# Moving constants and loads, adding a branch hint and a PSUM unit, and searching a new instruction order, in an attention and state-space kernel

## Chip, cores and metric

The kernel runs on one core of a Trainium2 chip. The metric is the device time of one execution in microseconds (us). The number given for a kernel is the median of its runs. A profile is one more execution, taken by the hardware profiler. Its span, from first to last instruction, is about 1.8 us shorter than the device time of the same kernel.

## The reference, cut to what matters

Two halves with separate inputs, concatenated along the last axis. All inputs are bf16, S = 2048 positions, D = 448.

```python
def _A_ref(x, wqkv, wo):          # sliding, dilated attention: 16 heads of 28, 8 keys at distance 0, 2, ... 14
    q, k, v = split_heads(x @ wqkv)
    logits = einsum("bhsd,bhswd->bhsw", q, gather(k)) * Dh ** -0.5     # masked where the position is negative
    o = einsum("bhsw,bhswd->bhsd", softmax(logits), gather(v))
    return merge_heads(o) @ wo

def _B_ref(x, Lambda, B, C, log_dt, Dskip):   # diagonal complex state space
    Lam_bar = exp(exp(log_dt) * Lambda)
    Bu = x @ (((Lam_bar - 1) / Lambda)[:, None] * B).T
    h[t] = Lam_bar * h[t - 1] + Bu[t]
    return 2 * real(h @ C.T) + x * Dskip

out = concatenate([_A_ref(...), _B_ref(...)], -1)
```

## The kernel before

The kernel is a list of work items ("nodes"), each with an estimated cost per engine, an earliest start and a rank. A small planner walks these estimates in time and gives each engine a fixed order. The ranks come from a search outside the kernel. For items that two engines can do (`"V"` is DVE, `"A"` is ACT), the planner also chooses the engine. So a change of costs, start times or ranks changes the order on every engine and moves items from one engine to another.

The loads at the head, all issued in this order:

```python
    V.memset(zz[:, 0:640], 0.0)                  # operand of the warm-up matmuls
    xbar_x(xA, xA2, 0, 128)                      # SP: transposing load of 128 columns of x
    ACT.dma_start(Wv[0:64, 3, :], ...)           # 56 KB
    ACT.dma_start(Wv[:, 0:3, :], ...)            # 336 KB
    xbar_x(xA, xA2, 128, 256)
    xbar_x(xA, xA2, 256, 384)
    xbar_x(xA, xA2, 384, 512)
    # ... four small vectors, on ACT and GpSimd ...
    for q in (1, 0):                             # K, then Q weights, on SP
        SP.dma_start(Wraw[:, 0:3, D * q:D * q + D], ...)
        SP.dma_start(Wraw[0:64, 3, D * q:D * q + D], ...)
    # ... six loads of B weights on SP ...
    xbar_x(xA, xA2, 512, 768)                    # the second half of x
    xbar_x(xA, xA2, 768, 1024)
    xbar_x(xB, xB2, 0, 512)
```

V is computed in nine blocks, Q and K in column pieces. The weights of Q and K are first copied to a padded layout, in four sets of five copies, each set on DVE or ACT as the planner decides:

```python
    def n_wp(e, q, z):                           # one set
        # ...
        f = V.tensor_copy if e == "V" else ACT.copy
        f(o[:, 0:3], i[:, 0:3])
        f(o[0:64, 3], i[0:64, 3])
        f(o[64:128, 3], i[0:64, 0])
        f(o[0:64, 4:7], i[64:128, 0:3])
        f(o[64:128, 4:7], i[0:64, 1:4])
```

GpSimd (POOL) builds constants (masks, ones, zeros). It also makes a one-element memset, the "tick", between the two parts of each V, Q and K unit, for which PE waits:

```python
    def relay(h):
        k = h["tick"] = G.memset(tick[:, 0:1], 0.0)
        behind(k, h["done"][0])
        behind(k, h["done"][1])
```

At the end come eight output blocks `y`, each with two halves (`pe0`, `pe1`) in one PSUM unit of two banks, their evictions and stores, a one-element matmul that checks the softmax sums, and a branch on its result around an exact version of the attention. It skips that part.

```python
        def pe0(e, ...):
            ps = h["ps"] = unit()
            # ... 11 matmuls into ps[:, 0]
        def pe1(e, ...):
            ps, hb, lo = h["ps"], hbuf(hf), 128 * (t % 4)
            # ... 11 matmuls into ps[:, 1]
    # ...
    bad = nc.values_load(flag[0:1, 0:1], min_val=0, max_val=128)
    main.close()
    with tc.If(bad > 0):
        exact_attention(tc, A_x, A_wqkv, A_wo, out)
```

## Time and profile before

| | before |
|---|---|
| device time, median of 3 runs | 144.92 us (143.94 to 145.28) |
| span of the profile | 142.9 us |
| PE busy | 128.0 us, 90% |
| PE idle from 5.4 to 22 us | 5.9 us |
| PE's end to the end of the span | 6.5 us |

The prediction below shows the totals, the PE and DVE slices and the gaps. Two more views of the kernel before complete them. The first is POOL's row in the slices of the page (40 equal slices of the span; each digit is the busy share in tenths). The second is the list of what PE waited for between 5 and 22 us (line, releaser, total us, times, longest).

```profile
POOL 6967585902000000000000000000000000000000
```

```profile
PE mm L532 <- DVE Kt L511: 2.7, 2, 1.8
PE mm L533 <- DVE Wv L495: 1.0, 1, 1.0
PE mm L533 <- DVE Wpad L505: 0.9, 1, 0.9
PE mm L532 <- DVE Wpad L501: 0.7, 1, 0.7
PE mm L532 <- DMA xA<-in_A_x_dram: 0.6, 1, 0.6
```

POOL is busy for the first eight slices (28 us) and nearly idle afterwards. All but one of PE's head waits end with DVE work: the eviction of K out of PSUM (`Kt`), the padded weight copies (`Wpad`) and the copies that complete V's weights (`Wv`). The last, 0.6 us, is for the first tile of x.

### The profile page before, as it was taken

The numbers are of one execution on the slowest core, as the hardware profiler recorded it, in microseconds if no ns is written. First come the engines' busy times: TensorE is split into PE (matmuls) and PEld (weight loads), VectorE is DVE, ScalarE is ACT, GpSimd is POOL, SyncE is SP. The second block draws the span as 40 slices with busy tenths as digits, with TensorE's granted clock in tenths as the row PEclk, the third lists the DMA queues.
The fourth block names the chain that finished last, engine by engine and source line by source line (L and its number), as shares of the span: only waits on it lengthen the run. The fifth ranks groups of instructions, "written<-read, shape, count | busy, mean of one in ns | idle before, by whom it ended". The sixth has DMA issues, their size and how long they took to land.

```text
span 142.9 us, 3792 instructions
## 1 busy us (share of the span) xinstructions
PE 128.0 (90%) x1537; PEld 71.5 (50%) x1542; DVE 108.0 (76%) x228; ACT 89.5 (63%) x117; POOL 23.4 (16%) x86
## 2 busy tenths in 40 slices
PE   6697649999999999999999999999999999999910
PEld 2142538766634645454544656465656555455510
DVE  0349999999886999999999998999999995300000
ACT  0228963699898766998877799866652345222220
POOL 6967585902000000000000000000000000000000
PEclk9999999999999999999999999999999999999997
DMA  3999999302977949133030030255341295521120
GB/s 54 279 203 279 203 159 207 58 0 50 120 155 146 242 94 187 37 68 61 0 61 0 0 63 0 47 141 168 82 93 64 70 186 189 196 69 64 64 70 8
DMA packets 40449, 15.15 MB, mean 106 GB/s; under 512 B 33004, under 2 KB 40364, under 8 KB 40428
## 3 DMA queue, kind: packets, MB, share of 16 engines
q1 hardware_dynamic: 39728, 14.23, 47.4%
q0 software_dynamic: 192, 0.23, 1.0%
q10 hardware_dynamic: 508, 0.40, 0.9%
q8 instruction: 14, 0.23, 0.7%
q14 instruction: 7, 0.06, 0.1%
HBM read 3.16 MB, written 3.67 MB: 48 GB/s over the span
## 4 chain that ended last, share of the span: by engine, by line
PE 66%; DVE 21%; DMA 3%; issue 3%; ACT 2%; ACTq 1%; POOL 0%; POOLq 0%
PE mm L532 22%; PE mm L754 10%; PE mm L890 8%; PE mm L897 7%; PE mm L892 4%; PE mm L852 4%; PE mm L714 4%; DMA Wv<-in_A_wqkv_dram 3%; DVE rs L788 3%; PE mm L533 2%; DVE ra L767 2%; DVE rb L768 2%; PE mm L692 2%; DVE Kt L511 2%; DVE O L721 2%
## 5 line engine op out<-in xcount | busy, mean ns | idle before, releaser
L702 ACT ACTIVATE P<-mm 128x896 bf16<-128x896 f32 (+1 forms) x36 | 31.5, 934 | 2.3 <-PE mm L696 2.3
L532 PE MATMUL mm<-xA,Wpad 64*128 64x256 bf16 (+1 forms) x168 | 27.2, 305 | 3.8 <-DVE Kt L511 2.7
L533 PE MATMUL mm<-xA,Wpad 64*128 64x256 bf16 (+1 forms) x168 | 27.0, 306 | 0.9 <-DVE Wpad L505 0.9
L509 ACT CAST ys<-mm 128x896 bf16<-128x896 f32 (+1 forms) x15 | 12.5, 857 | 23.2 <-PE mm L900 17.4
L754 PE MATMUL mm<-xB,WT 128*128 128x512 bf16 x93 | 22.2, 380 | 0.3
L540 POOL MEMSET tick<- 1x1 f32 x41 | 4.6, 111 | 95.3 <-PE mm L533 95.0
L532 PEld LDWEIGHTS <-Wpad 64*128 64x128 bf16 x168 | 15.1, 94 | 8.7 <-DVE Wpad L501 1.2
L533 PEld LDWEIGHTS <-Wpad 64*128 64x128 bf16 x168 | 14.7, 94 | 4.8 <-issue 3.6
L754 PEld LDWEIGHTS <-WT 128*128 128x128 bf16 x98 | 8.9, 98 | 10.6 <-issue 0.4
L533 PE MATMUL mm<-Wv,xA 64*128 64x448 bf16 x63 | 13.1, 349 | 1.0 <-DVE Wv L495 1.0
L532 PE MATMUL mm<-Wv,xA 64*128 64x448 bf16 x63 | 13.2, 350 | 0.7 <-DMA xA<-in_A_x_dram 0.6
L890 PE MATMUL mm<-C,h 128*128 128x448 bf16 x56 | 11.9, 353 | 0.3 <-ACT P L702 0.3
L897 PE MATMUL mm<-C,h 128*128 128x448 bf16 x56 | 11.9, 353 | 0.0
L509 ACT CAST Qt<-mm 128x512 bf16<-128x512 f32 (+1 forms) x11 | 7.9, 749 | 6.1 <-PE mm L533 5.9
L532 PE MATMUL mm<-wo,OT 64*128 64x448 bf16 x56 | 10.8, 349 | 0.0
L533 PE MATMUL mm<-wo,OT 64*128 64x448 bf16 x56 | 10.8, 349 | 0.0
L953 DVE TENSOR_SCALAR flag<-mm 1x1 int32<-1x1 f32 x1 | 0.1, 147 | 13.5 <-PE mm L950 13.5
L721 DVE TENSOR_TENSOR O<-mm,rcs 112x896 bf16<-112x896 f32 (+1 forms) x9 | 9.8, 1092 | 0.3
L509 ACT CAST u<-mm 128x1024 bf16<-128x1024 f32 (+1 forms) x7 | 6.3, 893 | 4.4 <-PE mm L754 4.4
L714 PEld LDWEIGHTS <-P 128*128 128x128 bf16 x288 | 8.2, 96 | 1.7 <-issue 0.8
L532 PEld LDWEIGHTS <-xA 64*128 64x128 bf16 x63 | 5.7, 94 | 6.6 <-issue 1.3
L714 PE MATMUL mm<-Vt,P 128*128 128x29 bf16 x288 | 8.7, 176 | 0.1
(175 smaller groups left out, 243.6 us busy)
## 6 DMA issues: line engine op xcount, KB each, us to landing
out_dram<-ys SPq DMA_DIRECT2D x15, 224.0 KB, 2.4
Wraw<-in_A_wqkv_dram SPq DMA_DIRECT2D x2, 336.0 KB, 4.4
wo<-in_A_wo_dram SPq DMA_DIRECT2D x2, 336.0 KB, 4.8
Wv<-in_A_wqkv_dram ACTq DMA_DIRECT2D x1, 336.0 KB, 4.4
natW<-in_B_B_re_dram SPq DMA_DIRECT2D x1, 336.0 KB
natW<-in_B_B_im_dram SPq DMA_DIRECT2D x1, 336.0 KB, 6.0
out_dram<-ys SPq DMA_DIRECT2D x2, 112.0 KB, 2.5
OT<-O SPq DMA_TRANSPOSE x9, 2.8
```

Source lines behind the costliest of these rows:

```text
L509: ACT.copy(o, i)
L532: x = PE.matmul(ps[:, a, 0:n], lhs(0, lo[i]), rhs(0, lo[i]), start=(i == 0), stop=(i == 6), skip_group_check=True)
L533: y = PE.matmul(ps[:, b, 0:n], lhs(64, hi[i]), rhs(64, hi[i]), start=(i == 0), stop=(i == 6), skip_group_check=True)
L540: k = h["tick"] = G.memset(tick[:, 0:1], 0.0)
L702: ACT.activation(P[:].rearrange("p s g q -> p g s q")[:, 2 * z:2 * z + 2, :, 0:n], h["s"][z][:, :, 0:4 * n].rearrange("p g (s q) -> p g s ...
L714: PE.matmul(av[:, par, 29 * hd:29 * hd + 29], hb_[par]["P"][:, hd // 4, hd % 4, :], Vt[:, par, b, hd, :], start=True, stop=True)
L721: V.tensor_tensor(O[0:n, :].rearrange("p (a h d) -> p a h d", a=2, h=H), avv[0:n, :, :, 0:DH], rc.unsqueeze(3).to_broadcast((n, 2, H, DH)) ...
L754: PE.matmul(ps[:, i, :], WT[:, j, 128 * m:128 * m + 128], xB[:, j, HALF * hf:HALF * hf + HALF], start=(j == 0), stop=(j == 6))
L852: PE.matmul(ps[0:n, i, 0:D], natW[:, m, D + 128 * k:D + 128 * k + n], lazy["C1"][:, m, :], start=(m == 0), stop=False, skip_group_check=True)
L890: PE.matmul(ps[:, 0, 0:D], hb[:, m, lo:lo + 128], lazy["C2"][:, m, :], start=(m == 0), stop=False, skip_group_check=True)
L892: PE.matmul(ps[:, 0, 0:D], xB[:, k, tk], Gm[:, k, :], start=False, stop=(k == 3), skip_group_check=True)
L897: PE.matmul(ps[:, 1, 0:D], hb[:, m, lo + 1:lo + 129], lazy["C1"][:, m, :], start=(m == 0), stop=False, skip_group_check=True)
```

## The change

The intent has four parts. (a) POOL's constants come after DVE's weight copies (earliest start 17 us, and cut into small pieces so that ticks fit between them), so that they no longer run beside those copies (beside a memset of POOL the same 128x672 copy took 1.50 and 0.84 us, apart from them 0.38). (b) All of x is loaded in eight tiles ahead of the B weights, so that PE has V blocks to do early. The Q and K weights go to ACT's queue. (c) The end: a prefetch hint for PE's branch, and a PSUM unit for each half of the last output block. (d) A new search of the ranks for these arrival times. Four C loads also move from POOL to SP, and two small vector loads from ACT to POOL (neither is shown in the diff).

```diff
-RANK = {"v": (67.97, 4.568), "q0": (138.6, -7.905), "q1": (-53.81, 27.558), "s": (-197.77, 32.213), ...
+RANK = {"v": (-66.31, 15.076), "q0": (294.15, -25.592), "q1": (-315.77, 68.252), "s": (340.5, 1.243), ...
     # (all 20 pairs differ)
+    ACT.dma_start(Wv[:, 0:3, :], ...)
     ACT.dma_start(Wv[0:64, 3, :], A_wqkv[384:448, 2 * D:3 * D])
-    ACT.dma_start(Wv[:, 0:3, :], ...)
-    xbar_x(xA, xA2, 128, 256)
-    xbar_x(xA, xA2, 256, 384)
-    xbar_x(xA, xA2, 384, 512)
+    for i in range(1, 4):
+        xbar_x(xA, xA2, 128 * i, 128 * i + 128)
     for q in (1, 0):
-        SP.dma_start(Wraw[:, 0:3, D * q:D * q + D], ...)
-        SP.dma_start(Wraw[0:64, 3, D * q:D * q + D], ...)
+        ACT.dma_start(Wraw[:, 0:3, D * q:D * q + D], ...)
+        ACT.dma_start(Wraw[0:64, 3, D * q:D * q + D], ...)
+    for i in range(4, 8):
+        xbar_x(xA, xA2, 128 * i, 128 * i + 128)
     # ... B weights ...
-    xbar_x(xA, xA2, 512, 768)
-    xbar_x(xA, xA2, 768, 1024)
-    xbar_x(xB, xB2, 0, 512)
+    for i in range(4):
+        xbar_x(xB, xB2, 128 * i, 128 * i + 128)
     # ...
-    gm = [node(f"gm{i}", {"G": c}, f, [], 3 + i) for i, (c, f) in enumerate(((1.3, g_m1), ...))]
-    g_1 = node("one", {"G": 1.3}, g_one, [], 10)
-    g_z = node("zer", {"G": 1.7}, g_zero, [], 11)
+    late = 17.0
+    for i, f in enumerate(gms):                  # 15 pieces
+        gm.append(node(f"gm{i}", {"G": 0.42}, f, gm[-1:], 4, at=late))
+    g_1 = [node(f"one{a}", {"G": 0.67}, ..., at=late) for a in range(2)]
+    g_z = [node(f"zer{i}", ..., at=late) for i in range(4)]
     # ... estimated costs and start times adjusted, the weight copies from 10.8/11.8 to 8.5/10.0 ...
         def pe0(e, ...):
-            ps = h["ps"] = unit()
+            if t == 6:
+                tc.mark_branch_hint_location("exact", engines=(mybir.EngineType.PE,))
+            ps = h[0] = h[1] = unit()
         def pe1(e, ...):
+            if t == 7:
+                h[1] = unit()
-    with tc.If(bad > 0):
+    with tc.If(bad > 0, label="exact"):
```

## The prediction

> **What bounds the kernel now.** I read the page's totals and slices first, then the busy time of each engine by stage, then the PE timeline where it has gaps, then DVE and POOL beside those gaps, and last the end of the span. From the page:
>
> ```profile
> span 142.9 us, 3792 instructions
> PE 128.0 (90%) x1537; PEld 71.5 (50%) x1542; DVE 108.0 (76%) x228; ACT 89.5 (63%) x117; POOL 23.4 (16%) x86
> ...
> PE   6697649999999999999999999999999999999910
> ...
> DVE  0349999999886999999999998999999995300000
> ...
> PE 66%; DVE 21%; DMA 3%; issue 3%; ACT 2%; ACTq 1%; POOL 0%; POOLq 0%
> ```
>
> PE is full from slice 7 to slice 37, and it alone is full in the last sixth. It has holes in the first six slices, and there DVE is full. The stages, cut at the end of the warm-up matmuls (5.4 us), at the last hole and at PE's last matmul:
>
> ```profile
> 5.40:22.00 16.60, 10.71 (x131) 6.50 (x131) 13.70 (x41) 9.94 (x18) 11.44 (x32) 1.00 1.09 219
> 22.00:136.40 114.40, 113.21 (x1398) 63.61 (x1400) 93.81 (x187) 77.33 (x96) 7.92 (x41) 1.00 0.43 92
> 136.40:142.90 6.50, 0.05 (x1) 0.00 (x0) 0.15 (x1) 0.97 (x2) 0.00 (x0) 0.86 0.15 43
> ```
>
> The columns are length, then PE, weight load, DVE, ACT, POOL. PE is idle 5.9 us in the first stage and 1.2 us in the second; 6.5 us follow PE's end. So there are about 12 us in all that are not matrix work after the warm-up, and half lie in the head. The holes (PE timeline, idle before and releaser in brackets):
>
> ```profile
> 7.40 0.35 PE L533 MATMUL mm<-Wv,xA 64*128 64x448 bf16 x1 [1.04 <-DVE Wv L495]
> 13.82 0.28 PE L532 MATMUL mm<-xA,Wpad 64*128 64x256 bf16 x1 [0.73 <-DVE Wpad L501]
> 14.96 0.28 PE L533 MATMUL mm<-xA,Wpad 64*128 64x256 bf16 x1 [0.86 <-DVE Wpad L505]
> 18.96 0.27 PE L532 MATMUL mm<-xA,Wpad 64*128 64x256 bf16 x1 [1.75 <-DVE Kt L511]
> 21.50 0.27 PE L532 MATMUL mm<-xA,Wpad 64*128 64x256 bf16 x1 [0.94 <-DVE Kt L511]
> ```
>
> The last four are one cause: PE ran out of V blocks (only four of nine, since only 512 columns of x were loaded early), and then waited for DVE, which had the padded weight copies and the PSUM evictions in one queue. What slowed DVE, DVE and POOL lines of the same stretch:
>
> ```profile
> 12.26 1.50 DVE L501 COPY Wpad<-Wraw 128x672 bf16<-128x672 bf16 x1
> 15.95 0.84 DVE L501 COPY Wpad<-Wraw 128x672 bf16<-128x672 bf16 x1
> 18.83 0.38 DVE L501 COPY Wpad<-Wraw 128x672 bf16<-128x672 bf16 x1
> 12.19 1.32 POOL L351 MEMSET Vt<- 128x288 bf16 x1
> 15.73 0.82 POOL L355 MEMSET P<- 128x256 bf16 x3
> ```
>
> The same copy takes 0.38 us alone and 1.50 or 0.84 us when a POOL memset began just before it.
>
> [...] the first copy ends at 13.76, 0.25 us after the memset's end at 13.51, although the copy itself needs 0.38. [...] PE's compare-and-branch at 137.26 lasts 3.42 us, those of ACT, POOL, DVE and SP 0.05 to 0.07. [...] the C loads that move from POOL to SP landed 8.3 us after issue[...], but nothing on the path waits for them.
>
> **The change, part by part.**
>
> *Start of V.* The large part of Wv is now issued first on ACT's queue. Before, it was issued at 1.42 and landed at 5.78, behind a 56 KB piece at 0.82. Swapped, it should land about 0.55 us earlier (the issue that it stood behind took 0.56). The three DVE shift copies (5.81 to 7.35) move with it, unless the first x tile, which PE took at 6.00, holds it. Gain 0.5.
>
> *Head.* Eight 128-column transposes of x come before the other operands, so all nine V blocks can run. A block is 14 matmuls, 7 pairs at 0.188 us, so 1.32 us, and x tiles come about as fast (four took 5.56 us to issue, 1.39 each). The built order interleaves V blocks with K and Q units (7 pairs at 0.11, 0.77 us), so PE waits neither for one nor for the other. The Wraw loads move to ACT's queue; the K part should land some 2 us earlier than now (issue about 2.0 and 4.4 us to landing, against 6.42), later if it shares bandwidth with x, so I take 8.5. The Q part is held behind a semaphore of Wv and comes about 10. The weight copies become two sets on DVE and two on ACT (before: three and one). A set on DVE without POOL costs 0.38 + 0.19 + 0.21 + 0.39 + 0.39 = 1.56; on ACT 0.74 + 0.38 + 0.38 + 0.75 + 0.75 = 3.0. DVE saves 6.9 - 2 x 1.56 = 3.8 us of busy time.
>
> I walked the new order by hand with these durations and four PSUM buffers. PE starts V at 6.85, has four V blocks until 12.1, three K units until 14, V4 until 15.9, waits 0.5 for a buffer that ACT frees after its second weight set, then runs to 28 with waits of 0.4, and 0.5 and 0.6 up to the first softmax. That is 2.0 us of waits. Before, the starts of the matmuls at the four holes (12.74, 13.82, 14.96; 16.94, 18.96; 20.29, 21.50) are 5.45 us apart; less ordinary spacing and with some small late starts, 5.4 lost. Gain 3.4.
>
> *Middle.* The matrix work itself is unchanged. The order has fewer V, K and Q units left as filler, because they were done earlier. ACT must do the 36 exponentials (31.5 us) and its evictions in about 5 us less; I count 54 us of ACT work in a 60 us stretch. DVE's list after the first rotation shrinks by 2.9 us (two evictions of 1024 columns at 1.22, one of 896 at 1.09, less 0.66 for one of 512), and its last h piece, 119.88 now against the use of h at 121.84, should be ready at about 115. So neither becomes the end bound, but with three engines over 90% full some new waits will appear. I take 0.6 lost.
>
> *Tail.* The last block's two halves get a PSUM unit each. Now the eviction of the first half waits for the last matmul:
>
> ```profile
> 136.43 0.97 ACT L509 CAST ys<-mm 128x448 bf16<-128x448 f32 x2 [2.70 <-PE mm L900]
> ...
> 136.99 0.84 SPq L908 DMA_DIRECT2D out_dram<-ys  x2
> ```
>
> With its own unit the first half leaves under the second half's matmuls, and the last store is issued one eviction earlier: gain 0.43 (second eviction begins 136.43 instead of 136.86). The hint: SP's closing waits begin when the last store has landed (140.77), and PE's long branch ends at 140.69, so the branch alone is hidden. But 13 of that store's 16 pieces land by 139.21 and three only at 140.17, 140.52 and 140.77, and three instruction fetches (16 KB for 1.07 us, 8 KB for 0.56 and 0.65) lie just then in the DMA records. If PE's fetch goes earlier, the stragglers partly vanish. At most 1.5 us; the two 8 KB fetches probably belong to other engines and stay; the hint stands in the built program at the very start of PE's stream, not at the seventh block, so it may be spent long before the branch. I take 0.6.
>
> *Sum.* 0.5 + 3.4 - 0.6 + 0.43 + 0.6 = 4.3 us; 144.92 - 4.3 = 140.6.
>
> **Rivals.** (1) DVE, not PE, is the true limit: the chain of waits runs through DVE from 10 to 21 and from 44 to 62 us. Then the head gain is given back between 40 and 90, and only DVE's own saving (3.8 + 2.9, less four V evictions at 1.09 moved to it) counts: 2.3 us or so, and with the tail 141.6. For: DVE busy 93.8 of 114.4. Against: in the second stage PE is idle 1.2 us only. (2) Bandwidth: x, Wv and Wraw together are 2.3 MB before 8.5 us, near 290 GB/s, and the busiest slices show 279. If x tiles and weights come 2 us later than I think, the holes stay as waits for DMA, and half the head gain goes: 142.5. (3) The hint is without effect or hidden: 141.2. (4) Everything goes well, the stragglers vanish (1.5) and no new waits appear: 139.1.
>
> **Range and chances.** The rivals against it are worth +0.6 to +2 each and the one in favour -1.5, so 140.6 with 138.6 to 142.6 eight times in ten; the three times of before are themselves spread by 1.3 us. Faster by 2% means below 142.02; only rival 2, or 1 with 3, lands above. Faster 0.87, same 0.12, slower 0.01.
>
> **What would show it.** Right: PE busy in 5.4 to 22 rises from 10.7 to over 14 us; no Wpad copy over 0.5 us of the 128x672 form on DVE; POOL's constants lie after 17 us; PE's last matmul ends near 133 (now 136.4); its branch is short; the last store lands less than 2.5 us after issue (now 3.3). Wrong: PE holes put down to x or Wraw transfers before 15 us (rival 2); PE idle in the 22 to 133 stretch of well over 2 us, behind ACT's exponentials or DVE's rotations (rival 1); a PE branch of 3 us (rival 3). If the head gain appears but PE's end does not move with it, the order, not the head, is what I misjudged.

The 0.6 for the hint was the author's estimate: the DMA records of the kernel before show four instruction fetches near the end (at 138.26, 138.31, 138.54 and 141.46 us) but not for which engine, so "PE's fetch" and its link with the late pieces of the store were a theory, here and in the expectations of e1 to e4.

## The result and the profile after

A ratio here is the mean time of one kernel's fast runs over the mean of the other's fast runs of the same rounds, so it is not quite the ratio of the medians quoted.

| | before | after |
|---|---|---|
| device time, median of 4 runs | 144.59 us | 139.31 us (138.83 to 141.16, the longest a slow run) |
| ratio, 95% interval | 1 | 0.962 (0.955 to 0.969) |
| span | 142.9 us | 137.1 us |
| PE busy, share | 128.0 us, 90% | 128.6 us, 94% |

The page of the changed kernel: totals, three rows of slices (PE, DVE, POOL), and the chain of waits by engine.

```profile
span 137.1 us, 3790 instructions
...
PE 128.6 (94%) x1536; PEld 72.0 (53%) x1542; DVE 104.7 (76%) x222; ACT 93.0 (68%) x123; POOL 21.4 (16%) x85
...
PE   6959999999999999979999999999999999999970
...
DVE  0646986999996999999999999899999999500000
...
POOL 6500148889400000000000000000000000000000
...
PE 68%; DVE 11%; ACT 10%; DMA 5%; issue 2%; SPq 1%; DVEq 0%; ACTq 0%
```

PE is full from the fourth slice on, but for one slice of 7 tenths. DVE's share of the chain falls from 21% to 11%. POOL's block of work now lies in slices 6 to 11 and leaves the first weight copies alone. The stages, cut at the same places as in the prediction (PE's end is now 132.90), with length, then busy time of PE, weight load, DVE, ACT and POOL:

```profile
5.40:22.00 16.60, 15.06 (x176) 8.51 (x176) 11.04 (x36) 11.74 (x20) 3.56 (x22) 1.00 1.02 219
22.00:132.90 110.90, 109.39 (x1357) 62.00 (x1357) 92.16 (x184) 80.77 (x103) 13.62 (x53) 1.00 0.45 94
132.90:137.10 4.20, 0.07 (x1) 0.00 (x0) 0.15 (x1) 0.53 (x1) 0.00 (x0) 0.95 0.19 61
```

The first row must not be read as matrix work alone, because the warm-up matmuls (`tab`) reach into it. The clock records show the full clock from 4.50 us on in the profile before and from 6.97 after, and until then matmuls take longer (V's first one 0.55 us before 6.97, later ones 0.35). So the warm-up ended at 5.43 and at 6.22 us (start and length; first line before, second after):

```profile
1.34 4.09 PE L962 MATMUL mm<-tab 128*128 128x512 bf16 x11 [1.34 <-DVE tab L283]
1.34 4.88 PE L954 MATMUL mm<-tab 128*128 128x512 bf16 x11 [1.34 <-DVE tab L283]
```

So 0.8 us of the 15.06 are warm-up. This is chance and not the change: e1, e2 and e3 below have the same head, and their warm-up ended at 5.63, 5.61 and 5.34. The sum without it, counted in the records from V's first matmul (6.00 before, 6.15 after): PE is idle for 5.33 us before and 1.54 after up to 22 us, so 3.79 less. From there to its end it is idle for 1.51 us instead of 1.19, 0.32 more. Its busy time in both together is 123.84 and 123.67, so about the same. With V's start 0.15 later, PE's end comes 3.5 us earlier (136.40 to 132.90). What follows it shrinks from 6.50 to 4.20, 2.30 us. Together that is 5.8 us, the difference of the spans.

The head in detail: first the list of what PE waited for between 5 and 22 us, then two weight copies from DVE's timeline and the first of POOL's moved memsets from its timeline.

```profile
PE mm L516 <- DMA xA<-in_A_x_dram: 1.4, 1, 1.4
```

```profile
7.01 0.39 DVE L485 COPY Wpad<-Wraw 128x672 bf16<-128x672 bf16 x1 [0.56 <-DMA Wraw<-in_A_wqkv_dram]
15.65 0.38 DVE L485 COPY Wpad<-Wraw 128x672 bf16<-128x672 bf16 x1
...
18.87 0.20 POOL L324 MEMSET mst<- 32x128 bf16 x1
```

One wait is left, for the second tile of x. It landed at 9.03 us instead of 6.89, because the Q and K weights are now moved at the same time (h1 below shows this). Both 128x672 copies on DVE take 0.38 to 0.39 us. The evictions of the last output block, on ACT:

```profile
131.43 0.53 ACT L493 CAST ys<-mm 128x448 bf16<-128x448 f32 x1 [1.18 <-PE mm L881]
132.91 0.53 ACT L493 CAST ys<-mm 128x448 bf16<-128x448 f32 x1 [0.94 <-PE mm L891]
```

The first half leaves 1.5 us before PE's end; only the second half follows it. PE's branch, which lasted 3.42 us, lasts 0.39. The last store is issued at 133.47 and all its 16 pieces have landed at 135.18, 1.71 us later, where before three pieces came up to 3.31 us after the issue.

### The profile page after: what moved, and what is told of

It is laid out like the page before. It is cut to its first block, busy times and chain, and to the rows that moved or that the text cites. A ratio compares the mean times of both kernels' runs of the same rounds, so it can differ in the third digit from the quotient of the medians.

```text
span 137.1 us, 3790 instructions
## 1 busy us (share of the span) xinstructions
PE 128.6 (94%) x1536; PEld 72.0 (53%) x1542; DVE 104.7 (76%) x222; ACT 93.0 (68%) x123; POOL 21.4 (16%) x85
## 4 chain that ended last, share of the span: by engine, by line
PE 68%; DVE 11%; ACT 10%; DMA 5%; issue 2%; SPq 1%; DVEq 0%; ACTq 0%
PE mm L516 18%; PE mm L742 14%; PE mm L879 8%; PE mm L888 8%; PE mm L702 5%; DMA xA<-in_A_x_dram 5%; PE mm L881 4%; PE mm L839 4%; PE mm L680 3%; ACT P L690 3%; PE mm L684 2%; DVE tmpB L437 2%; DVE Vt L495 2%; ACT tab L446 1%; ACT tab L440 1%
## 5 line engine op out<-in xcount | busy, mean ns | idle before, releaser
L516 PE MATMUL mm<-xA,Wpad 64*128 64x256 bf16 (+1 forms) x168 | 26.8, 305 | 0.3 <-ACT P L690 0.3
L493 ACT CAST ys<-mm 128x896 bf16<-128x896 f32 (+1 forms) x16 | 13.5, 861 | 20.0 <-PE mm L891 13.9
L517 PE MATMUL mm<-xA,Wpad 64*128 64x256 bf16 (+1 forms) x168 | 26.8, 305 | 0.0
L524 POOL MEMSET tick<- 1x1 f32 x41 | 5.2, 128 | 94.1 <-PE mm L517 93.7
L516 PE MATMUL mm<-Wv,xA 64*128 64x448 bf16 x63 | 13.8, 357 | 1.5 <-DMA xA<-in_A_x_dram 1.4
L517 PE MATMUL mm<-Wv,xA 64*128 64x448 bf16 x63 | 13.6, 354 | 0.0
L776 DVE TENSOR_TENSOR_SCAN rs<-p_r,ini,rv 128x512 bf16<-128x512 f32 x7 | 8.6, 1270 | 0.0
```

Source lines behind the costliest of these rows:

```text
L493: ACT.copy(o, i)
L516: x = PE.matmul(ps[:, a, 0:n], lhs(0, lo[i]), rhs(0, lo[i]), start=(i == 0), stop=(i == 6), skip_group_check=True)
L517: y = PE.matmul(ps[:, b, 0:n], lhs(64, hi[i]), rhs(64, hi[i]), start=(i == 0), stop=(i == 6), skip_group_check=True)
L776: V.tensor_tensor_scan(h["s"][:, i], p["r2"][:, k:k + 1].to_broadcast((128, HALF)), h["v"][:, i], 0.0 if hf == 0 else ini[:, m:m + 1], ALU ...
```

## The experiments

Twelve kernels ran, four to a job (e, h, and o with h5), with five rounds each beside the kernel before; e and h ran on the same chip, the last job on another. All gave correct results. The changed kernel itself ran in rounds of its own, earlier. In the tables the ratio is to the kernel before of the same rounds, from fast runs alone. The medians are over all six runs of a kernel, and e2, e3 and h3 had one slow run each.

### The end of the span: hint and last PSUM unit (e1 to e4)

The edits, each on the changed kernel, and for e4 on the kernel before:

```diff
# e1_no_hint
-            if t == 6:
-                tc.mark_branch_hint_location("exact", engines=(mybir.EngineType.PE,))
# e2_no_split
-            if t == 7:
-                h[1] = unit()
-        n1 = node(f"z{t}", ..., alloc="mm" if t == 7 else None)
+        n1 = node(f"z{t}", ...)
-                      frees=[(n1 if a else n0, 0)])
+                      frees=[(n0, 0)])
# e3_neither: both
# e4_before_hint, on the kernel before
+            if t == 6:
+                tc.mark_branch_hint_location("exact", engines=(mybir.EngineType.PE,))
-    with tc.If(bad > 0):
+    with tc.If(bad > 0, label="exact"):
```

e1: 

> The changed kernel without the hint; every engine's order stays, PE has one instruction less. Theory A (the hint moves PE's 16 KB instruction fetch out of the closing 4 us, and the last store gains because nothing is in its way): PE's compare-and-branch goes from 0.39 back to about 3.4 us, and with it the fetch, about 1 us after the branch. The branch would then end near 137.2, after SP begins its closing waits (135.0), so it becomes the bound itself: span about 138.0 to 138.6 instead of 137.1, time about 140.2 to 140.8. Theory B (the hint is hidden, the gain of the tail is the separate PSUM unit alone): branch 3.4 us, but span and time within 0.3 us of the changed kernel (139.0).

e2: 

> The changed kernel with the hint, but with both halves of the last block in one PSUM unit as before; all orders are the same. Theory A: the last eviction begins 0.43 us later, the store is issued 0.5 us later and moves its data while the two 8 KB fetches run, so its last piece lands 0.5 to 1.0 us later: time +0.5 to +1.0. Theory B: all of the tail's 2.3 us is lost, time about +1.5 or more.

e3: 

> The changed kernel without hint and without the separate unit: the closing part as in the kernel before behind the new order. PE's last matmul still at about 132.9, then 6.5 us as before: span 139.4, time 141.2 to 141.5. If hint and unit are worth 2.3 us together, the difference to the changed kernel is that; if the sum of what the two single removals cost is less or more than this, they overlap.

e4: 

> The kernel before with the hint alone, orders the same. PE's branch 0.4 us instead of 3.4. Theory A: the 16 KB fetch leaves the last store's way, the last piece lands at 140.2 to 140.5 instead of 140.8 because the two 8 KB fetches of other engines stay: time -0.3 to -0.6. Theory B, hidden: within 0.2 us of before. If all three stragglers go: -1.5.

| | median us | ratio, 95% interval | span |
|---|---|---|---|
| e1, split without hint | 140.38 | 0.972 (0.969 to 0.975) | 138.4 |
| e2, hint without split | 140.96 | 0.976 (0.972 to 0.980) | 139.1 |
| e3, neither | 141.22 | 0.977 (0.972 to 0.982) | 139.7 |
| e4, before with hint | 144.48 | 1.000 (0.997 to 1.004) | 142.6 |

What sets the end is read from single records of the traces: PE's branch, the last store's issue and landing, and the first instruction fetch (8 or 16 KB, the records name no engine for it) that follows (all us):

```
                 PE branch           last store   last piece   first fetch   after the
                 from      lasts     issued       landed       starts        store's issue
before           137.26    3.42      137.46       140.77       138.26        0.80
e3 neither       134.14    4.16      134.34       138.09       135.13        0.79
e2 no split      133.63    0.40      133.84       137.46       134.63        0.79
e4 before, hint  136.75    0.39      136.95       140.41       137.90        0.95
e1 no hint       133.92    3.34      133.60       135.31       134.93        1.33
after            133.83    0.39      133.47       135.18       134.84        1.37
```

Three things follow. First, the hint works wherever it is: 0.39 to 0.40 us instead of 3.3 to 4.2. Second, it is worth next to nothing alone, because the last pieces of the store land nearly as late as the branch ended (140.77 and 140.69 us before, 140.41 in e4). In e4 a 16 KB fetch still starts 1.15 us after the start of PE's branch, and pieces of the store come late as before. Third, the late pieces vanish with the split, not with the hint. With the split, the last store is issued 0.3 us before PE's branch; without it, 0.2 us after. Where the first fetch starts 0.79 to 0.95 us after the store's issue, pieces come late (before, e2, e3, e4); where it starts 1.33 us or more after it, none does (e1, after). The later kernels agree: h4, without the split, has 1.08 us and late pieces, and all of the others have 1.34 us or more and none. Where pieces come late, it is the last three of 16, and the last of them lands 3.3 to 3.8 us after the issue; otherwise all pieces of a store of this size land within 1.8 us. This is a regularity over all fourteen traces (in o2 the last store is a larger one, of 224 KB).

The DMA records show what separates the two groups. The last store of 112 KB moves in 128 packets of 896 bytes. In the five kernels with late pieces, 81 to 128 of these packets began after the first fetch had begun, and 8 to 16 of them took over 60 ns, up to 391, where the usual packet takes about 42. In the nine others all of them had begun before the first fetch. Whether the fetches slow the packets, and by what way, no run shows. A rival is not tested apart: without the split, the last two stores are also issued only 0.47 us after one another, with it 1.48 or more. The trace of o2 speaks against it, for there the packets of the last two stores follow one another without a pause and no piece is late.

So the two parts need one another: in these six traces the span ends 1.1 to 2.2 us after the later of the store's landing and the end of PE's branch, and each part works on one of the two: the hint shortens the branch (to 0.39 and 0.40 us), and the split brings the landing sooner (1.7 us after the issue instead of 3.3 to 3.8). From e3, the hint alone moves the median of the fast runs by 0.15 us and the split alone by 0.7, within or near the intervals. The traces separate them better, counted from PE's last matmul to the end of the span: 6.5 us before, 6.7 in e4, 6.4 in e3, 6.2 in e2, 5.3 in e1 and 4.2 in the changed kernel (its profile is from its own rounds). So in the new kernel the hint alone takes about 0.1 us, the split alone 1.1 and both 2.2. In e1 theory A's figures came out right: once the late pieces are gone, PE's branch, which ends at 137.26, is what ends last. Its reason did not: the hint does not move the fetch after the branch out of the store's way. The 16 KB fetch that follows PE's branch starts at 134.93 in e1 and at 134.95 with the hint; what the hint removes is a second one, at 138.02. In e2 the size that theory B named is nearer: the split is worth much more than one eviction of 0.43 us.

### The head: weights, table load, constants (h1 to h4)

```diff
# h1_weights_behind_x, on the changed kernel: Wraw loads on SP, behind the first four x tiles
-        ACT.dma_start(Wraw[...], ...)            # both, for Q and K
+        SP.dma_start(Wraw[...], ...)
# h2_table_load_first, on the changed kernel: a tiny Exp at the head of ACT
+    warm = t_([1, 2], F32, "warm")
+    ACT.activation(warm[:, 0:2], zz[0:1, 0:2], ACTF.Exp)
# h3_pool_early, on the changed kernel: constants early, order of the other engines unchanged
+        moved = [n for n in order if n["name"].rstrip("0123456789") in ("gm", "one", "zer", "rcs")]
+        for i, n in enumerate(moved):
+            n["start"] = 5.72 + 0.45 * i
# h4_before_pool_late, on the kernel before: constants late, order of the other engines unchanged
+        moved = [n for n in order if n["name"].rstrip("0123456789") in ("gm", "one", "zer", "rcs")]
+        moved += [n for n in order if n["name"] in ("dgE", "dgO")]
+        for i, n in enumerate(moved):
+            n["start"] = 19.3 + 1.3 * i
```

h1: 

> The changed kernel, its four Wraw loads put back on SP's queue behind the first four x tiles, as before; the orders of PE, DVE, POOL and ACT's compute are the same. In the changed kernel the second x tile landed at 9.03 us (before: 6.89) and PE waited 1.4 us for it. Theory X (the early Wraw loads share bandwidth with x and delay it, and that wait is paid in full): x tiles at about 6.9, 7.4 and 8.3 again, no wait for x, PE's end 1.0 to 1.5 us earlier, time -1.0 to -1.5 against the changed kernel. Theory Y (the wait only changes its name: the weights then land at 10.2 and 12.8 and the copies come after them): PE waits for Wpad at about 12 to 13 us for 1 to 2 us, time within 0.5 us, or slower.

h2: 

> The changed kernel with one tiny activation ahead of the Wraw loads on ACT, so that ACT's function table load (1.28 us) lies ahead of them and they are issued about 1.5 us later; else the same. Theory X: the second x tile lands at about 8.0 instead of 9.0, the wait for it shrinks from 1.4 to about 0.5; the first Wraw part lands near 8.5, still before PE needs it (12): time -0.5 to -1.0. Theory Y: no change within 0.3 us.

h3: 

> The changed kernel with POOL's constants put back early, spread between its relays as before; all other orders the same. Theory P [...]: the DVE copies of Wpad at 7 to 10 and 15.6 to 17.2 us go from 0.2 to 0.4 to up to 1.5 us each, DVE falls behind by 1 to 2 us, PE gets holes for Wpad: time +0.5 to +1.5. Theory R (the copies have slack now, because PE has V blocks to do): the copies are slower, but the time is within 0.3 us.

h4: 

> The kernel before with POOL's constants after its C loads (from about 20 us), spread between relays; all other orders the same. Theory P: the Wpad copies at 12.3 and 16 take 0.38 us instead of 1.50 and 0.84, DVE is about 1.9 us ahead at 20 us, the four PE holes shrink by 1 to 1.5 us in sum: time -0.8 to -1.5. Rival: DVE's copies are faster but PE waits for the later relays or the PSUM evictions instead: within 0.4 us of before.

| | median us | ratio, 95% interval | span |
|---|---|---|---|
| h1 | 138.60 | 0.958 (0.955 to 0.961) | 136.8 |
| h2 | 139.10 | 0.964 (0.960 to 0.967) | 136.8 |
| h3 | 140.93 | 0.974 (0.971 to 0.978) | 139.0 |
| h4 | 144.78 | 1.002 (0.998 to 1.005) | 143.0 |

PE's waits between 5 and 22 us in h1:

```profile
PE mm L516 <- DVE Vt L495: 0.4, 1, 0.4
PE mm L516 <- DMA xA<-in_A_x_dram: 0.2, 1, 0.2
```

With the weights behind four x tiles, the second tile lands at 7.64 us instead of 9.03 and the wait for x falls from 1.4 to 0.2 us. PE is busy for 15.79 us of the stage instead of 15.06 (the warm-up is the same in both). PE's last eviction comes 0.3 us earlier (132.63), so more than half of these 0.7 us is given back further on. Theory X was right about the wait but named 1.0 to 1.5 us. This is the fastest kernel. Against the changed kernel, which ran in other rounds, the 0.7 us between the medians (0.4 with its slow run left out) is near the spread of that kernel's few runs, so a gain of h1 over it is likely but not proven. The weights moved beside x were the cause of the wait that is left in the changed kernel.

PE's waits of the same stretch in h2:

```profile
PE mm L518 <- DMA xA<-in_A_x_dram: 1.0, 2, 0.6
PE mm L519 <- ACT Wpad L491: 0.5, 1, 0.5
PE mm L518 <- ACT Kt L495: 0.3, 1, 0.3
```

The table load ran early, but it also delayed three of the four weight issues on ACT's queue (Q's large part from 4.34 to 7.86 us). The wait for the second x tile shrank to 0.5 us (the other 0.6 is the first tile, which the longer warm-up hides in the changed kernel's profile), and waits for ACT's copies and evictions came in its place. PE's idle time from V's first matmul to 22 us is 1.54 us in both. The time is that of the changed kernel within its interval.

In h3, the first two copies of the second weight set on DVE, and then what PE waited for between 5 and 22 us:

```profile
15.94 1.17 DVE L488 COPY Wpad<-Wraw 128x672 bf16<-128x672 bf16 x1
17.03 0.59 DVE L489 COPY Wpad<-Wraw 64x224 bf16<-64x224 bf16 x1
```

```profile
PE mm L519 <- DMA xA<-in_A_x_dram: 2.5, 3, 1.4
PE mm L519 <- DVE Kt L498: 1.0, 1, 1.0
PE mm L519 <- DVE p_th L371: 0.2, 1, 0.2
```

With POOL's memsets again beside the second set, the copy that took 0.38 us takes 1.17, and the wait for the K eviction behind it returns. Counted from V's first matmul (6.15 us in both), PE is idle for 2.97 us up to 22 us instead of 1.54, and the two waits for DVE are 1.3 of these 1.4 us. Its last eviction comes 1.9 us later. The longer waits for x in this list (2.5 us, in the changed kernel 1.4) are no cause: 0.8 of them is the first tile, which the longer warm-up hides in the changed kernel's profile, and the second tile landed at 8.76 us, not later than 9.03. The first set, at 7.5 to 9.9 us, beside POOL's small masks of 32 rows, was not slowed (its 128x672 copy began 0.10 us into a memset of 32 rows that took 0.19, and took 0.39), although theory P had named both sets. What in POOL's work slows the copy was not shown: it took 0.84 and 1.50 us (before) and 1.17 (h3) beside memsets of 128 rows, but the copy of 1.50 ended 0.25 us after the memset, less than the 0.38 that it takes apart from them. POOL's spans are rough, and no run separated its kinds of instruction. The place of the constants is thus a true part of the gain in the new order: 1.3 us of waits for DVE, and 1.6 us between the medians (of different rounds).

In h4 the constants were moved in the old order. What PE waited for between 22 and 42 us (0.2 us in the kernel before):

```profile
PE mm L536 <- POOL tick L544: 2.5, 3, 1.1
```

All three 128x672 copies on DVE became short (0.38 to 0.39 us) and DVE ran about 3 us ahead at 18 us, but the time did not change. (Two smaller copies, beside the issues of POOL's C loads, still took 0.43 and 0.68 us instead of 0.20 and 0.39.) The constants, in their old large pieces, then stood in POOL's queue in front of ticks, and PE waited for those. PE's idle time falls by 2.8 us up to 22 us and rises by 2.3 after it. This is the gain given back as a new wait, as the rival had it. The finer pieces are meant to avoid it; no run tests them alone.

### The order (o1 to o3) and a last attempt at the end (h5)

```diff
# o1_new_kernel_old_ranks: the changed kernel with the RANK table of before
# o2_old_kernel_new_ranks: the kernel before with the RANK table of the changed one
# o3_old_ranks_late_x: as o1, and
-    for i in range(4, 8):
-        xbar_x(xA, xA2, 128 * i, 128 * i + 128)
-    for i in range(4):
-        xbar_x(xB, xB2, 128 * i, 128 * i + 128)
+    xbar_x(xA, xA2, 512, 768)
+    xbar_x(xA, xA2, 768, 1024)
+    xbar_x(xB, xB2, 0, 512)
-        return (5.9, 6.9, 7.8, 8.9, 10.2, 11.5, 12.8, 14.1)[(t - 1) // 128]
+        return (5.9, 6.9, 7.8, 8.9, 18.0, 18.0, 20.0, 20.0)[(t - 1) // 128]
# h5_weights_behind_x_split_eviction: as h1, and the last half evicted by two engines
+            n2 = [node(f"ye{t}{a}{q}", {q: c}, ...) for q, c, lo, hi in (("A", 0.22, 0, 240), ("V", 0.28, 240, D))]
```

o1: 

> The changed kernel with the rank table of the kernel before; loads, constants, hint and last unit stay as changed. Theory O (the newly searched order is a part of the gain, since an order found for the old arrival times leaves PE waiting when the operands come at other times): new waits of PE, at least 1 us of them together, in the head or the middle, and 140.3 to 142 us. Theory L (the placement of loads and constants does it, the order only spends the small rest): within 0.5 us of the changed kernel, so 138.8 to 139.8, and PE's busy time between 5.4 and 22 us about 15.

o2: 

> The kernel before with the rank table of the changed one alone. Theory O: the new order fits only the new arrival times, so here it brings nothing or loses: 144 to 147 us against 144.5 of before, with PE's busy time between 5.4 and 22 us at 10.7 or less. Rival (the new order is better in itself): 142 to 143.5.

o3: 

> As o1, but the second half of x (rows 512 to 1023) is loaded where it was before, in two pieces of 256 columns behind the B weights, and planned for 18 and 20 us as before; the order of PE, DVE, ACT and POOL is built exactly as in o1, only the queue of loads differs. Theory X (loading all of x ahead is a part of the gain): PE waits for x tiles by 2 us or more around 13 to 20 us, and the time is 1.5 us or more above o1. Theory Y (with the old order PE gets to the second half of x only after 18 us, so early x is of use only together with the new order): within 0.5 us of o1, with no wait for x over 0.5 us beyond those of o1.

h5: 

> As h1 (the Wraw loads on SP's queue behind four x tiles, 138.6 us), and the eviction of the very last output half is split by columns between ACT (240) and DVE (208), so that the last store can leave sooner. An eviction of 448 columns takes about 0.45 us now; half of it about 0.25. If the last store sets the end, the time falls by 0.1 to 0.25 us to 138.35 to 138.5; if a fixed closing part or PE's branch sets it, it stays at 138.6.

| | median us | ratio, 95% interval | span | PE busy | PE idle |
|---|---|---|---|---|---|
| o1, new placement, old ranks | 153.35 | 1.064 (1.058 to 1.069) | 151.4 | 134.6 | 16.8 |
| o2, old placement, new ranks | 150.37 | 1.041 (1.037 to 1.045) | 148.5 | 131.2 | 17.3 |
| o3, as o1 with late x | 157.65 | 1.091 (1.086 to 1.095) | 156.1 | 138.2 | 17.9 |
| h5 | 138.88 | 0.960 (0.958 to 0.962) | 137.3 | | |

(PE idle is the span less PE's busy time; it is 8.5 us in the changed kernel.)

The theory that the order matters was right, but its size was far off: 140.3 to 142 was expected for o1 and it took 153.35. Either half of the change alone makes the kernel slower than before; only together do they make it faster. What was swapped is the table of ranks, from which the planner then makes its order. A fresh search of ranks for the old placement was not run, so how much a further search alone would bring stays open. The PE and clock rows of o1's slices (PEclk is the TensorE clock granted, in tenths of full speed), and then PE's longest waits in it:

```profile
PE   6979599968989999999999828999999999999990
...
PEclk9999999999999999999999955599999999999999
```

```profile
PE mm L680 <- ACT u L493: 2.5, 1, 2.5
PE mm L517 <- ACT Wpad L489: 1.9, 1, 1.9
PE mm L516 <- DVE Vt L495: 1.4, 1, 1.4
```

The old ranks give three of the four weight sets to ACT, where a set takes 3.0 us; PE waits 1.9 us for the third. A later hole of 2.5 us, from 88.0 to 90.5 (behind ACT, which waited for DVE), lies in a stretch of half clock from 87.6 to 97.9 us; the clock fell just before it, after two shorter holes of 0.4 and 0.6 us. The 14.3 us between the spans of o1 and the changed kernel are 8.3 us more idle time and 6.0 us more busy time, and PE had the same work. The clock records hold two rates, 0.5 and 1.0, and the stretches of half clock lasted 10.2 us here and 3.4 and 6.8 us in o3. What brings the half clock was not shown. In the 3.41 us (the length of the shortest such stretch) before it fell, the profile has PE busy for 2.30 us (o1, at 87.61) and for 1.18 (o3, at 19.26), and in the kernel before it stayed full after 1.66 us of 3.41 (18.15 to 21.56), so PE's busy time in the profile doesn't decide it. An estimate from the clock records: PE is busy for 7.17 of the 10.24 us at half clock, so the half rate cost at most 3.6 of the 6.0 us. The rest has another cause, which was not followed; PE's busy time rose by 2.6 us over the changed kernel's in o2 too, without any half clock in the middle.

Against the kernel before, o2's span is 5.6 us longer: 2.4 us more idle and 3.2 us more busy time of PE, and the latter was not explained. Its new waits are mainly for ticks (2.2 us in seven waits) and for V evictions on ACT (1.3 us). One wait of 1.3 us for a normalisation on DVE comes to that, and it ends with an attention output block of 896 columns instead of a `y` half.

o3 gave no answer on early x. Its only difference from o1 should have been the second half of x, but the table load of ACT, and with it the first weight set, came 3.4 us later, released by a transfer of x (first view, ACT's timeline; the bracket holds the idle time before and its releaser; the second is the clock row of the slices):

```profile
8.88 0.47 ACTq L293 DMA_DIRECT2D Wraw<-in_A_wqkv_dram  x1
9.39 1.28 ACT L484 ACT_TABLE_LOAD   x1 [9.39 <-DMA xA<-in_A_x_dram]
```

```profile
PEclk9969959999599999999999995599999999999999
```

In o1 the last of the four weight issues on ACT's queue went at 5.50 and the table load began at 6.00; in o3 the issue was held to 8.88. Which of ACT's waits changed in the build was not followed further. The clock records of o3 have four stretches of half clock, 17.1 us in all, against 10.2 in o1. PE never waited for the late tiles themselves, so both theories miss; what loading all of x ahead is worth by itself stays open.

In h5 the two evictions of the last half did not run side by side:

```profile
132.88 0.36 ACT L493 CAST ys<-mm 128x240 bf16<-128x240 f32 x1 [0.94 <-PE mm L891]
133.27 0.38 DVE L495 CAST ys<-mm 128x208 bf16<-128x208 f32 x1 [13.75 <-ACT ys L493]
```

DVE was released by ACT's eviction, so 0.36 + 0.38 us in a row replaced 0.53. The last store left 0.80 us after the first eviction's start instead of 0.56, and the time is that of h1 or a little more. The expectation of 138.35 to 138.5 missed for that reason. Whether two engines can read that bank at once was not tried.

## Why the prediction was right, and where it was off

The prediction of 140.6 us (138.6 to 142.6) holds 139.31, and the main mechanism is as it said. Its steps in order:

- *Start of V and head, 0.5 + 3.4.* Measured 3.6: 3.79 us less idle time of PE up to 22 us, less the 0.15 by which V starts later. Wv's large part landed at 4.32 instead of 5.79, which is 1.5 us earlier and not 0.55. V's first matmul did not gain, since the first x tile held it, as the prediction allowed; what went is the wait of 1.04 us behind DVE's copies of Wv. PE's busy time in the stage is 15.06, or 14.25 without the warm-up, where over 14 was named, no copy of the named form is over 0.5 us, and POOL's constants start at 18.87. That this term fits is in part luck: the walk had 2.0 us of waits, for a buffer that ACT frees and further on up to the first softmax, and the trace has one of 1.4 us before 22 us, for an x tile, which the walk had not. h3 shows that the place of the constants is part of the gain in the new order; h4, with the old order and the old large pieces, gained nothing from it.
- *Middle, 0.6 lost.* Measured 0.3, all of it idle time. PE's end, predicted near 133, is 132.9.
- *Tail, 0.43 + 0.6.* This is the mis-sized term: 2.30 us instead of 1.03. The prediction took the split of the unit as one eviction, and gave the late pieces to the hint, because PE's fetch would go earlier. No fetch is seen to: a 16 KB fetch starts 1.1 us after the start of PE's branch with the hint and 1.0 without it (after, e1). The runs show that with the store 0.5 us further ahead of the instruction fetches the late pieces are gone, with or without the hint (e1 against e2). "The branch alone is hidden" was right for the kernel before (e4: 1.000), but once the pieces came in time the branch would have been the end (e1: 1.1 us over the changed kernel's median). The doubt that the hint is spent too early at the start of PE's stream was unfounded: it stands at 0.90 us, and the branch at 133.83 lasts 0.39 us.
- *Rivals.* DVE as the true limit: no, its share of the chain halved and PE's end moved. Bandwidth: right in kind, since the one wait left is for an x tile that landed 2.1 us later than before, but it cost 1.4 us and not half the gain; h1 confirms the cause. Hint without effect or hidden: true without the split (e4, e2 against e3), not with it (e1). The fourth, 139.1 with the late pieces gone, came nearest.
- *Loads issued by POOL.* The C loads took 8.3 us from issue to landing (median) on POOL's queue in the kernel before, and 2.9 to 3.8 us on SP's in the changed one. But in h4, still on POOL, they took only 4.4 to 5.4, so the queue is not the whole of it.
- *What the prediction did not see.* It treated the new order as a means to use the early operands, and gave it no term of its own. o1 and o2 show that for these two tables of ranks it is not a term but a condition: with the old table the same placement takes 14 us more.

## What to carry to other kernels

Before two profiles are compared stage by stage, look at where the warm-up ended in each: here it differed by up to 0.9 us between kernels with the same head, as much as some effects that were looked for. When an order was searched for certain arrival times, don't judge a changed load or constant under the old order: move both, or read a bad result as one of the order. Two parts of an ending can hide one another, so look at all that ends last (a store's last pieces, a branch) and test them together. When a wait goes away, look for the engine queue in which the moved work now stands ahead of something short.
